# Sliding-window attention into a squared-ReLU MLP on one core: group 3 by seven products, one exponential a score bank, wider masks and sums, and a new order list

## The chip, the core and the metric

The kernel runs on one core of one Trainium2 chip. The metric is device time in microseconds (us): the median of several executions, and for one profiled execution also its span, from the first to the last instruction that the profile shows. The engines are named as in the profile: PE (TensorE, matmul), PEld (its weight loads), DVE (VectorE), ACT (ScalarE), POOL (GpSimd, here the issuer of the loads that cast) and SP (SyncE, here the issuer of the DMA transposes and of the stores).

## What is computed

The attention has 8 batches, 8 heads, 576 positions and head size 64, with a linear distance bias per head and a window of 128 positions. Its output, 4608 tokens of width 512, goes through an MLP of width 2048 with a squared ReLU. Inputs and output are float32.

```python
scores = scale * np.matmul(q, k.transpose(0, 1, 3, 2))
rel = pos[:, None] - pos[None, :]
bias = slopes[:, None, None] * (-np.abs(rel).astype(np.float32))[None, :, :]
mask = (rel >= 0) & (rel < window)
scores = np.where(mask, scores + bias[None], -1000000000.0)
...
attn = np.exp(scores)
attn = attn / (np.sum(attn, axis=-1, keepdims=True) + 1e-09)
return np.matmul(attn, v).astype(np.float32)
...
h = x @ w_in
r = np.maximum(h, 0.0)
g = r * r
return (g @ w_out).astype(np.float32)
```

## The kernel before, in words

**Blocks and groups.** The tokens are cut into 36 blocks of 128 queries (0 to 35; blocks 14, 21, 28 and 35 hold the last 64 positions of two batches). Each block goes through attention and leaves 128 columns of `xT`, the transposed input of the MLP. Four blocks make a group of 512 tokens; there are nine groups (0 to 8), and group g needs blocks 4g to 4g + 3. The first eight blocks are the first 128 positions of the batches and see only themselves.

**One block.** POOL loads K and Q (task `lkq`, `load_block`, L540 to L548) and V (`lv`, L550) with a cast to bf16 into rings of 4 and 9 tiles. From block 8 on, SP transposes K and Q by DMA into a ring of 7 (`kqT`, L592); a tile of `kq` is free again when that transpose has landed. PE makes the scores (`s`, L676) into four PSUM banks. ACT takes the exponential (`e`, L711, and `ex`, L719), DVE multiplies by a mask that holds the bias and the window (`m`, L725 to L734). PE multiplies by V in two halves (`pv`, L835), DVE divides by the sums (`r`, `n`, L854 and L859), and from block 8 on SP transposes the result by DMA into `xT` (`x`, L866). In a full block the scores of one head have three strips of 64 columns in each half of the partitions. One `e` takes the two outer strips of two heads (256 columns), one `ex` the middle strip (128 columns), so a bank has two exponentials; the middle strip is copied to two places by the mask's multiplication, so four heads have two masks of 512 elements.

**The way up** (x times w_in, ReLU, square). Groups 0 to 2 go in pieces (`unit`, `u`, L982), group 3 in 16 steps of four matmuls with 512 columns (`fc_step`, `fc`, L1002). Groups 4 to 8 (`G_UP = 4`) take each of four units (256 of w_in's columns and their partners 1024 further on) by seven products in place of eight (`up_product`, `f`, L1087): each product is four matmuls with 256 columns, on sums and differences of w_in's parts (`us`) and of x's parts (`ut`). Two PSUM banks serve a unit: X takes products 1, 6, 7, 4 and Y takes 2, 5, 3. The bank of product 1 is copied to Y (`s1.g.u`, the seed), and product 2 adds onto it there. Copies of X and Y after products 6 and 5 are parked in SBUF (`s2`, `s5`), and DVE adds them later (`c22`, `c12`, L1112).

**The way down** (g times w_out) of group 0 is direct (`o`, L1172). Groups 1 to 8 have seven products of 2 x 8 matmuls with 256 columns (`product`, `p`, L1261) on sums of the squared tile (`S1` to `S4`, `prepare`, two halves of 1024 elements each, L1391). After product 1 its bank is copied to an SBUF tile (`s1`), and DVE adds product 2's bank to it (`c11`, L1319).

**Order.** Every instruction group is a named task. `ORDER` lists all tasks by hand; the program walks the list and emits them in that order, so each engine runs its tasks in the list's order and waits for what a task needs. A `+` behind a name takes the second engine that the task allows. `SLACK`, `FILL` and the prices of the tasks enter only how many filling matmuls stand in planned gaps of the first 30 us. PSUM's eight banks are four rings: `h` (2), `ox`, `oy` (1 each) and `a` (4).

Of the kernel before, what the change touches and what calls it, by code (L numbers as in the profile page):

```python
# [9 lines left out]
AF = mybir.ActivationFunctionType  # L10
# [10 lines left out]
N_PVH = 2  # L21
# [3 lines left out]
SLACK = {"kqT": 4500.0, "v": 2300.0, "x": 2700.0}  # L25
FILL = 0.7
# [4 lines left out]
TP, XP = "h", "h"  # L31
# [8 lines left out]
G_A = 8  # L40
XR = 12
OSB = 5
LAST = 128
G_UP = 4
# [6 lines left out]
UNSEEDED = ((7, 1), (7, 3))  # L51
SQ_G = 0
SIZE = {"kq": 4, "v": 9, "kqT": 7, "P": 3, "x": 6}
# [15 lines left out]
    o0.0.3 ev4.1.0 ws0.3 lv6 tp5.0 squ0.5.0 tp5.1 lkq8 ev5.0.0 o0.1.3 ev5.1.0+ mask1.1 mask1.3 mask0.1 mask0.5 tp6.0
    oe0.1.0+ s4 lv7 oe0.0.0+ o0.3.0 e4.0 ws1.0 lkq9 mask1.4 e4.3 tp6.1 o0.3.1 e4.1 ev6.1.0+ ev6.0.0 one0.7 o0.2.0  # L70
    m4.0 lv8 e4.2 m4.1 one1.8 m4.3 squ0.5.1+ pv4.0 tp7.0 m4.2 lkq10 tp7.1 r4.0 ev7.0.0 n4.0 pv4.1 kqT8 pv5.0 pv5.1
    ev7.1.0 o0.2.1 r5.0 r5.1 r4.1 n5.0 lkq11 n5.1 o0.3.2 st0.0.0 n4.1 s6 kqT9 xp5.0 lv9 e6.0 xp4.0 x5.0+ o0.2.2
    x4.0+ e6.3 lv10 one1.6 one1.0 m6.0 u1.0.0 e6.2 m6.3 e6.1 one0.6 u1.0.3 reluu1.0.0 m6.1 one1.3 m6.2 pv6.0 ws1.1
    u1.0.5 reluu1.0.3 lkq12 squ1.0.0 pv6.1 r6.0 u1.0.7 reluu1.0.5 n6.0 r6.1 us3.0 u1.0.6 n6.1 reluu1.0.7 squ1.0.5
    mask0.0 kqT11 pv7.0 squ1.0.7 pv7.1 reluu1.0.6 u1.0.2 us2.0 r7.1 squ1.0.3+ r7.0 n7.0 u1.0.1 squ1.0.6+ kqT10 n7.1
    reluu1.0.2 lkq13 o0.3.3 reluu1.0.1 squ1.0.2 mask0.6 xp6.0 mask0.2 s8 x6.0+ lv11 ws1.3 xp7.0 e8.0 u1.0.4 oe0.3.0+
    e8.3 lv12 ex8.1 x7.0 o0.2.3 one1.2 ex8.2 e8.2 reluu1.0.4 u1.1.1 st0.3.0 ws1.2 e8.1 st0.1.0 ex8.3 ws0.2 u1.1.4
    ex8.0 kqT12 reluu1.1.1 mask0.7 s9 squ1.1.1 reluu1.1.4 us3.1 u1.1.5 squ1.0.1 e9.0 m8.0 e9.2 oe0.2.0+ lkq14 ex9.3
    u1.1.0 ex9.0 reluu1.1.5 m8.1 ex9.1 squ1.1.4 p1.1.0 squ1.0.4+ m8.3 one1.4 m9.1 reluu1.1.0 u1.1.2 squ1.1.5 e9.1
    one1.1 m8.2 kqT13 squ1.1.0 pv8.0 reluu1.1.2 u1.1.3 r8.0 n8.0 ex9.2 e9.3 lkq15 u1.1.6 m9.2 reluu1.1.3 m9.0 S1.1.0  # L80
# [1378 lines left out]
```

## Time and profile before

| what | value |
|---|---|
| median of the runs | 291.29 us (290.59 to 291.85, 3 runs) |
| the profiled execution, its own time | 292.82 us |
| its span | 290.6 us |
| PE busy | 282.0 us, 97% |
| PEld, weight loads | 231.2 us, 80% |
| DVE busy | 233.6 us, 80% |
| ACT busy | 212.3 us, 73% |
| POOL busy | 103.9 us, 36% |
| moved by DMA | 39.67 MB, mean 137 GB/s |

The busy time of an engine leaves overlaps of its own instructions out; the mean time of one instruction in the lists by line does not, so many of them times their mean is more than their busy time. The chain that ended last is followed back from the last instruction, at each step to what released it. A wait is put down to the engine or DMA that came last.

### The profile page before, as it was taken

To read this page: it belongs to the slowest core of one execution; us is meant where nothing else is said; L and a number is where in the kernel's file an instruction comes from. 1 tells how busy PE (TensorE), PEld (TensorE's weight loads), DVE (VectorE), ACT (ScalarE), POOL (GpSimd) and SP (SyncE) were. 2 spreads that over 40 slices of the span, in tenths; PEclk is the share of its full clock that TensorE was granted. 3 is DMA by queue.
4 is the path that set the end of the run, shared out by engine and by line. 5 is a ranking of instruction groups with operands and counts; after the bars stand their busy time and mean duration, and the time that the engine had idled before them with its cause. 6 is when DMAs were issued, how large, how long until landed. Compare 5 with 4: busy or idle time off the path is not lost.

```text
span 290.6 us, 9452 instructions
## 1 busy us (share of the span) xinstructions
PE 282.0 (97%) x3785; PEld 231.2 (80%) x3785; DVE 233.6 (80%) x628; ACT 212.3 (73%) x521; POOL 103.9 (36%) x132
## 2 busy tenths in 40 slices
PE   8899999999999999999899999999999999999994
PEld 4678746888888987558788889898888988888884
DVE  4554187789958897878799999999999996989853
ACT  3766765887479873778579899899989867675820
POOL 8942497448470434624717097340000000000000
PEclk9999999999999999999999999999999999999999
DMA  8999999999999999999999999999830201300144
GB/s 147 161 198 205 203 168 156 181 179 155 151 170 142 132 153 145 158 144 171 157 182 151 187 165 126 165 167 244 131 71 25 76 18 38 126 2 0 56 117 138
DMA packets 159915, 39.67 MB, mean 137 GB/s; under 512 B 142336, under 2 KB 159360, under 8 KB 159872
## 3 DMA queue, kind: packets, MB, share of 16 engines
q0 software_dynamic: 104432, 18.10, 88.8%
q1 hardware_dynamic: 54640, 20.33, 44.0%
q10 hardware_dynamic: 800, 0.66, 0.8%
q8 instruction: 29, 0.48, 0.7%
q14 instruction: 14, 0.11, 0.1%
HBM read 36.70 MB, written 9.44 MB: 159 GB/s over the span
## 4 chain that ended last, share of the span: by engine, by line
PE 78%; DMA 15%; DVE 2%; ACT 1%; POOL 1%; issue 1%; POOLq 0%; DVEq 0%
PE o L1261 27%; PE h L1087 19%; PE h L982 12%; DMA vt<-in_v_dram 8%; DMA kqT<-kq 7%; PE o L1172 5%; PE pv L835 5%; PE s L676 4%; PE h L1002 1%; PE wm L575 1%; PE tp L608 1%; POOL kq L546 1%; ACT kqf L403 1%; PE o L1348 1%; PE s L781 1%
## 5 line engine op out<-in xcount | busy, mean ns | idle before, releaser
L938 ACT ACTIVATE rt<-h 128x512 bf16<-128x512 f32 (+1 forms) x103 | 60.6, 594 | 26.1 <-PE h L982 9.0
L1261 PEld LDWEIGHTS <-g 128*128 128x128 bf16 x624 | 59.6, 98 | 7.8
L1261 PE MATMUL o<-w_out_sb,g 128*128 128x256 bf16 x512 | 63.6, 273 | 0.0
L711 ACT ACTIVATE P<-s 128x256 bf16<-128x256 f32 (+1 forms) x120 | 46.6, 426 | 11.0 <-PE s L676 11.0
L546 POOL DMA_DIRECT2D kq<-in_k_dram x32 | 27.1, 850 | 67.8 <-DMA kqT<-kq 67.0
L982 PE MATMUL h<-xT,w_in_sb 128*128 128x256 bf16 (+1 forms) x432 | 46.6, 261 | 0.2 <-ACT rt L938 0.2
L953 DVE TENSOR_TENSOR g<-rt 128x512 bf16<-128x512 bf16 (+1 forms) x85 | 34.6, 416 | 11.6 <-ACT rt L938 11.5
L982 PEld LDWEIGHTS <-w_in_sb 128*128 128x128 bf16 x432 | 37.4, 98 | 5.5 <-issue 0.3
L951 ACT ACTIVATE g<-rt 128x512 bf16<-128x512 bf16 (+1 forms) x60 | 36.6, 624 | 3.6 <-DVE rt L1120 3.2
L1087 PE MATMUL h<-xT,w_in_sb 128*128 128x256 bf16 x240 | 34.4, 273 | 0.0
L1087 PEld LDWEIGHTS <-w_in_sb 128*128 128x128 bf16 x320 | 30.4, 98 | 4.1 <-issue 0.3
L1261 PE MATMUL o<-wsum,sums 128*128 128x256 bf16 x256 | 31.1, 273 | 0.0
L552 POOL DMA_DIRECT2D vt<-in_v_dram x32 | 27.2, 868 | 9.0 <-PE pv L835 7.5
L859 DVE TENSOR_TENSOR x<-pv,rec 128x256 bf16<-128x256 f32 x72 | 28.5, 416 | 0.9
L835 PEld LDWEIGHTS <-P 128*128 128x128 bf16 x544 | 23.4, 98 | 5.7 <-DMA vt<-in_v_dram 1.4
L546 POOL DMA_DIRECT2D kq<-in_q_dram x32 | 27.4, 863 | 0.0
L1261 PEld LDWEIGHTS <-sums 128*128 128x128 bf16 x256 | 24.7, 98 | 3.0
L403 ACT ACTIVATE osb<-o 128x512 f32<-128x512 f32 x29 | 17.3, 602 | 11.4 <-DMA out_dram<-osb 5.3
L719 ACT ACTIVATE P<-s 128x128 bf16<-128x128 f32 x96 | 24.1, 304 | 0.0
L1112 DVE TENSOR_TENSOR rt<-h,vf 128x512 bf16<-128x512 f32 x30 | 20.5, 688 | 4.2 <-PE h L1087 1.9
L1087 PE MATMUL h<-ut,kqf 128*128 128x256 bf16 x160 | 23.5, 273 | 0.0
L835 PE MATMUL pv<-vt,P 128*128 128x65 bf16 x416 | 21.2, 193 | 1.7 <-DMA vt<-in_v_dram 1.5
(97 smaller groups left out, 462.0 us busy)
## 6 DMA issues: line engine op xcount, KB each, us to landing
out_dram<-osb SPq DMA_DIRECT2D x53, 128.0 KB, 3.9
kq<-in_k_dram POOLq DMA_DIRECT2D x31, 128.0 KB, 7.1
kq<-in_q_dram POOLq DMA_DIRECT2D x31, 128.0 KB, 7.2
vt<-in_v_dram POOLq DMA_DIRECT2D x24, 128.0 KB, 7.5
w_out_sb<-in_moe_w_out_dram POOLq DMA_DIRECT2D x4, 512.0 KB, 14.8
w_in_sb<-in_moe_w_in_dram POOLq DMA_DIRECT2D x3, 512.0 KB, 12.1
vf<-in_v_dram POOLq DMA_DIRECT2D x8, 128.0 KB, 6.2
out_dram<-osb SPq DMA_DIRECT2D x4, 256.0 KB, 6.6
```

What stands on the lines that cost most here:

```text
L546: nc.gpsimd.dma_start(view(kq[s_kq[m].idx], i)[rows], from_)
L552: nc.gpsimd.dma_start(tile_of(s_v[m])[rows, :, 0:D], from_)
L711: nc.scalar.activation(o, s, AF.Exp, bias=0.0, scale=scale)
L719: nc.scalar.activation(Pt[sP.idx][:, w, 1, early], s, AF.Exp, bias=0.0, scale=scale)
L835: nc.tensor.matmul(sv.tile[:, hi * (D + 1):(hi + 1) * (D + 1)], prob, tile_of(s_v[mk])[:, h, 0:D + 1], start=mk == parts[0][2], stop=mk == m)
L859: nc.vector.tensor_tensor(o, heads(sv)[:, :, 0:D], sr.tile.unsqueeze(2).to_broadcast([n, 4, D]), op=ALU.mult)
L938: nc.scalar.activation(srt.tile[:, 0:n], slot.tile[:, 0:n], AF.Relu, bias=0.0, scale=1.0)
L951: nc.scalar.activation(o, i, AF.Square, bias=0.0, scale=1.0)
L953: nc.vector.tensor_tensor(o, i, i, op=ALU.mult)
L982: nc.tensor.matmul(slot.tile[:, f * w:(f + 1) * w], w_in_sb[:, cc, fc * 128:(fc + 1) * 128], xT[:, cc, lo % (XR * 128):lo % (XR * 128) + w ...
L1087: nc.tensor.matmul(slot.tile[:, j * 256:j * 256 + 256], a, b_, start=fresh and j == 0 and c == 0, stop=c == 1, skip_group_check=True)
L1261: nc.tensor.matmul(slot.tile[:, z * 256:z * 256 + 256], stationary(c), moving(c), start=fresh and z == 0 and c == 0, stop=c == F - 1, skip ...
```

## The change

- `G_UP` goes from 4 to 3: group 3 goes up by seven products too, six groups in all.
- A full block's scores go through one exponential of 384 columns a bank, all three strips at once, into a raw tile of the new ring `E` (2 tiles). One multiplication for four heads then reads the raw tile twice over (the view `strips`: columns 0 to 127 and 64 to 191 of each head), multiplies by both masks and writes 1024 elements to `P`. `P` has 2 tiles instead of 3, `osb` 4 instead of 5. `ex` is gone.
- The sums `S1` to `S4` of groups 1 to 7 are made whole (2048 elements) in place of two halves; group 8 keeps the halves.
- Way down: product 1's bank is copied to the second PSUM bank, and product 2 adds onto it; `c11` becomes a copy out of that bank. All units of the way up are seeded (`UNSEEDED` is gone).
- The four PSUM rings become eight single banks. A task that takes a bank of kind `any` has its number behind a colon in the list; score blocks with four banks take banks 4 to 7.
- The list is new throughout (1676 tasks in place of 1814), with it the order of POOL's loads and SP's transposes and stores.

The core of the diff, and of the list the places that the text below speaks of:

```diff
-SLACK = {"kqT": 4500.0, "v": 2300.0, "x": 2700.0}
-FILL = 0.7
+SLACK = {"kqT": 3000.0, "v": 2300.0, "x": 1500.0}
+FILL = 0.85
...
-OSB = 5
+OSB = 4
...
-G_UP = 4
+G_UP = 3
...
-SIZE = {"kq": 4, "v": 9, "kqT": 7, "P": 3, "x": 6}
+SIZE = {"kq": 4, "v": 9, "kqT": 7, "P": 2, "E": 2, "x": 6}
...
-    n3.0 w_out2 e3.1 u0.0.1 x2.0+ pv3.1 u0.3.0 reluu0.0.1 r3.1 squ0.0.0+ n3.1 squ0.0.1 xp3.0 squ0.1.0 reluu0.3.0
...
-    r15.1 u2.1.5 n15.1 x14 squ2.1.0+ S1.2.1 s16 reluu2.1.1 S3.2.1 x15 p2.2.0 reluu2.1.5 S2.2.1 e16.0 p2.1.1 squ2.1.5
...
-    m18.2 fc3.0 r16.1 r16.0 n16.0 lkq26 pv17.0 m18.3 relufc3.0 fc3.7 r17.0 n17.0 n16.1 pv17.1 relufc3.7 fc3.5 r17.1
...
+    us0.2 S1.2.0 s15 s1_2:2 pv14.0:1 e15.0 pv14.1:0 S2.2.0 e15.2 p2.2.0 e15.1 e15.3 p2.2.1 r14.0 S3.2.0 s16 n14.0
+    p2.6.0 m15.1 r14.1 m15.0 e16.0 e16.1 e16.2 n14.1 p2.5.0:1 e16.3 pv15.0:5 pv15.1:6 us2.2 p2.6.1 m16.0 x14 r15.0
+    p2.5.1 lv21 n15.0 r15.1 n15.1 m16.1 x15 s17 s2_2 p2.7.0 p2.7.1 e17.0 S4.2.0 e17.2 c11_2 e17.1 lkq20 s5_2+ p2.3.0
+    c22_2 kqT19 kqT21 e17.3 pv16.0:0 r16.0 m17.1 s18 n16.0 p2.3.1 m17.0 e18.0 e18.2 c12_2 e18.3 p2.4.0 kqT23
+    pv16.1:4 m18.1 e18.1 r16.1 m18.0 pv17.0:5 pv17.1:0 n16.1 st2.2.0 st2.3.0 p2.4.1 s3_2 pv18.0:6 f3.0.1:7 f3.1.1:4
...
-    psum_bufs = {"h": 2, "ox": 1, "oy": 1, "a": 4}
+    psum_bufs = {f"b{i}": 1 for i in range(8)}
...
+    def strips(s):
+
+        e = Et[s.idx][:, :, 0:128].rearrange("p h (t q) -> p h t q", t=2)
+        return bass.AP(tensor=e.tensor, offset=e.offset, ap=[*e.ap[:-1], [1, 128]])
...
-        sS = [Slot("a") for _ in range(4)]
+        sS = [Slot(f"b{4 + i}") for i in range(4)]
...
+        sE = Slot("E" if full else "P")
+        sP, sR = Slot("P") if full else sE, Slot("E")
...
-            cols = 256 if (i % 2 and not diag) or kind == "full" else 512
+            cols = 384 if full else 256 if i % 2 and not diag else 512
...
+                s = sS[i].tile[:, 0:cols]
+                if full:
+                    o = Et[sE.idx][:, 2 * i:2 * i + 2].rearrange("p j q -> p (j q)")
...
-            if kind == "full":
-                def expo_x(i=i, w=w):
-                    s = sS[i].tile[:, 0:384].rearrange("p (c s q) -> p c s q", c=2, s=3)[:, :, 1]
-                    nc.scalar.activation(Pt[sP.idx][:, w, 1, early], s, AF.Exp, bias=0.0, scale=scale)
...
-                if i % 2:
-                    nc.vector.tensor_tensor(p[:, :, 1:3], p[:, :, 2:3].to_broadcast([128, 4, 2, 64]), mk[:, :, 1:3], op=ALU.mult)
-                else:
-                    nc.vector.tensor_tensor(p[:, :, 0:4:3], p[:, :, 0:4:3], mk[:, :, 0:4:3], op=ALU.mult)
+                nc.vector.tensor_tensor(Pt[sP.idx][:, g], strips(sE)[:, g], masks[:, g], op=ALU.mult)
...
-        fresh = p in (1, 2, 5)
+        fresh = p in (1, 5)
...
-        after = {6: "s1", 7: "s2", 3: "s5", 4: "c22"}.get(p)
+        after = {2: "s1", 6: "s1", 7: "s2", 3: "s5", 4: "c22"}.get(p)
...
         if p == 1:
-            snap("s1", [])
+            Y = st["slot"]["Y2"]
+
+            def seed():
+                bank(Y, "o")
+                copy(st["s1"], Y.tile, slot.tile)
+            st["s1"] = plan.add({"ACT": act(512), "DVE": dve_p(512)}, key, seed, both, [Y], [], name=f"s1_{g}")
         elif p == 2:
-            combine("s1", lambda o: nc.vector.tensor_tensor(o, slot.tile, o, op=ALU.add), both + [st["s1"]], [slot],
-                    0, 0, "c11")
+            snap("c11", [slot])
+            store("c11", st["c11"], 0, 0)
...
+        nq = 1 if g == NG - 1 else 2
+        for q in range(2 // nq):
+            qs = range(q * nq, q * nq + nq)
+            c, d = slice(4 * q, 4 * q + 4 * nq), slice(8 + 4 * q, 8 + 4 * q + 4 * nq)
```

The order of POOL's loads from block 16 on is, before: lkq16 lkq17 lkq18 lv15 lv18 lkq19 lkq23 lv16 lkq20 lv17 lkq21 lv19 lkq22 lv22 lkq26 lv20 lkq25 lkq24 lv21; after: lkq16 lv13 lv14 lkq17 lkq18 lv16 lv15 lv17 lv18 lkq19 lkq21 lv19 lkq23 lv21 lkq20 lkq22 lv22 lv20 lkq25 lkq26 lkq24.

More of the change, by code (lines that the diff above doesn't have):

```diff
@@ L262, in order @@
                     slots_at = max(slots_at, u[-n].freed)
-                    s.prev = u[-n]
+                if s.seed and not (u and u[-1].full):
+                    raise RuntimeError(f"{name}: its bank was not written as a whole before")
                 u.append(s)
@@ L1033 @@
     up_st = {}
-    t_parked, seeds = {}, []
+    t_parked = {}
     def prepare_up(g, key):
@@ L1422 @@
     kernel.plan = done
-    for X, Y in seeds:
-        if not (Y.prev and Y.prev.full):
-            raise RuntimeError("a bank is seeded that was not written as a whole before")
     with tc.manual_schedule():
```

355 lines of the change are left out of this document (170 added, 185 removed).

## The prediction

> **What bounds the kernel now.** I read the page first, to see which engine is never idle.
>
> ```profile
> span 290.6 us, 9452 instructions
> ...
> PE 282.0 (97%) x3785; PEld 231.2 (80%) x3785; DVE 233.6 (80%) x628; ACT 212.3 (73%) x521; POOL 103.9 (36%) x132
> ...
> DMA  8999999999999999999999999999830201300144
> ...
> PE 78%; DMA 15%; DVE 2%; ACT 1%; POOL 1%; issue 1%; POOLq 0%; DVEq 0%
> ```
>
> TensorE (PE) is busy for 282.0 of 290.6 us, but DMA is near full for the first 28 of 40 slices and holds 15% of the chain. So I ask, with busy time by stretch, where PE's missing 8.6 us lie.
>
> ```profile
> 0.00:20.00 20.00, 17.36 (x226) 12.06 (x227) 10.65 (x41) 11.80 (x28) 16.04 (x26) 1.00 1.30 165
> 80.00:100.00 20.00, 19.74 (x356) 17.04 (x355) 14.64 (x46) 17.00 (x47) 7.90 (x9) 1.00 1.75 157
> 100.00:120.00 20.00, 19.54 (x292) 14.65 (x288) 17.21 (x44) 12.66 (x40) 8.89 (x11) 1.00 2.21 136
> 140.00:160.00 20.00, 18.70 (x291) 16.10 (x290) 17.64 (x52) 14.96 (x41) 11.49 (x14) 1.00 1.96 163
> 160.00:180.00 20.00, 19.71 (x295) 16.93 (x294) 19.71 (x53) 18.84 (x52) 12.33 (x16) 1.00 1.73 162
> 240.00:260.00 20.00, 20.00 (x185) 17.93 (x184) 16.93 (x36) 15.04 (x29) 0.00 (x0) 1.00 0.20 61
> 280.00:290.60 10.60, 6.95 (x72) 6.16 (x69) 2.80 (x6) 2.25 (x4) 0.00 (x0) 1.00 0.43 128
> ```
>
> The columns are length, then PE, weight loads, VectorE (DVE), ScalarE (ACT), GpSimd (POOL), clock, DMA. PE lacks 2.64 us in the start, 3.65 in the end, and 0.26 + 0.46 + 1.30 + 0.29 = 2.3 between. The clock is 1.00 throughout. Does a busy PE mean a full PE? The chain of waits gives runs of matmuls without a gap:
>
> ```profile
> 71.20 0.47 PE s L676 x32
> ...
> 76.73 0.48 PE pv L835 x16
> 77.21 0.88 PE o L1261 x8
> ...
> 115.67 0.86 PE h L1002 x4
> ...
> 116.78 1.73 PE h L1002 x8
> ...
> 147.61 0.87 PE h L1087 x8
> ```
>
> Eight matmuls with 256 columns take 0.87 us (0.109 each), four with 512 take 0.86 (0.216 each): the array is streaming. The kernel is bound by the number of columns that PE streams, plus about 2.6 us of start and 2.3 us of waits.
>
> ```profile
> L1087 PEld LDWEIGHTS <-w_in_sb 128*128 128x128 bf16 x320 | 30.4, 98 | 4.1 <-issue 0.3
> ```
>
> A weight load takes 98 ns and fits under either pitch; in 240 to 260 us the loads are busy 17.93 of 20, 98 of each 109 ns.
>
> The Trainium skill, "Perfetto Trace Analysis", section "Identifying the Most-Contended Engine", says to judge PE's headroom by the busy share of weight loads and not of matmuls. By that rule 80% would leave a fifth; the pitches above leave almost nothing, since a 512-column matmul covers its load twice over.
>
> **The change, part by part.**
>
> *Group 3 by seven products.* Sixteen steps of four 512-column matmuls become four units of seven products with four 256-column matmuls: 64 x 0.216 = 13.8 us against 112 x 0.109 = 12.2. **-1.6 us** of PE, on the path.
>
> The Trainium skill, "TensorE: Matmul & The Clock Gate", section "Back-to-back issue gap", speaks against this: in a stream of load-matmul pairs it gives about 81 ns for 128 columns and 131 for 512. On a straight line that is an estimate of 98 ns for 256, and group 3 would go from 8.4 to 11.0 us, 2.6 us dearer. The rows above (0.216 and 0.109) disagree, so I keep -1.6.
>
> *Exponentials, masks, sums, copies.*
>
> ```profile
> L711 ACT ACTIVATE P<-s 128x256 bf16<-128x256 f32 x104 | 38.1, 399 | 8.8 <-PE s L676 8.8
> L719 ACT ACTIVATE P<-s 128x128 bf16<-128x128 f32 x96 | 24.1, 304 | 0.0
> L711 ACT ACTIVATE P<-s 128x512 bf16<-128x512 f32 x16 | 9.0, 600 | 2.1 <-PE s L676 2.1
> L732 DVE TENSOR_TENSOR P<-P,masks 128x512 bf16<-128x512 bf16 x48 | 19.6, 418 | 2.9 <-ACT P L719 2.8
> L734 DVE TENSOR_TENSOR P<-P,masks 128x512 bf16<-128x512 bf16 x48 | 19.6, 416 | 3.6 <-ACT P L711 3.6
> L1391 DVE TENSOR_TENSOR sums<-g 128x1024 bf16<-128x1024 bf16 x16 | 11.0, 685 | 0.5 <-ACT g L951 0.2
> L1319 DVE TENSOR_TENSOR osb<-o,osb 128x512 f32<-128x512 f32 x8 | 5.4, 678 | 0.1
> L403 ACT ACTIVATE h<-h 128x512 f32<-128x512 f32 x16 | 9.4, 588 | 5.9 <-PE h L1087 5.3 <-DVE rt L1120 0.4 <-DVE rt L1112 0.2
> L1112 DVE TENSOR_TENSOR rt<-h,vf 128x512 bf16<-128x512 f32 x30 | 20.5, 688 | 4.2 <-PE h L1087 1.9 <-ACT g L951 0.8 <-ACT vf L403 0.6
> L1120 DVE TENSOR_SCALAR rt<-rt 128x512 bf16<-128x512 bf16 x27 | 7.9, 298 | 0.2
> ```
>
> ACT: 96 pairs of 399 + 304 ns become 96 instructions with 384 columns. None is in the trace; it lies between the 256 and the 512 form (399 and 600), and I take the middle, 500. That is 67.5 - 48 = 19.5 us less by durations; by busy totals, which leave overlaps out (38.1 x 96/104 + 24.1 = 59.3 against 96 x about 0.465 = 44.6), 14.7. Added: the eight c11 copies that move to ACT, and one more 512-wide instruction in group 3 (8 relus and 9 copies for 16 relus), 9 x 0.6 = 5.4. ACT net about -9 us.
>
> DVE: 96 masks of 0.417 become 48 of 1024 elements; their nearest row is the 1024-wide sum, 0.685: 39.2 - 32.9 = -6.3. The new operand reads overlapping strips; at half the speed (417 grows by 269 ns per 512 more, so about 1.2 us) they would cost 48 x 0.54 = +26 instead. I take 0.685, since the old masks already read 64-wide strips, one of them repeated, at 417, the same as whole tiles. Sums of groups 1 to 7: 28 pairs of 0.685 become 28 of about 1.22, -4.1. The eight c11 additions leave, -5.4. Group 3 adds eight additions at 0.688, eight relus at 0.298, four differences at about 0.42 and three copies that the list gives DVE, about 2.1: +11.7. DVE net about -4.
>
> What are these worth? **0**: neither engine sets the end, and PE hides them while there is other PE work in line. A gain is bounded by PE's waits on them (below). A loss: a 2048-wide sum is ready 0.54 us later, and product 5 waits for it; products 1 and 2 (4 x 0.87 = 3.5 us) stand ahead and cover the two sums (2.4). Without that cover it is about 1 us in each of seven groups.
>
> *Product 2 of the way down is seeded.* It now waits for a copy of 0.59 us after product 1; in the queue behind it stands all later PE work. The new list puts other work between: least in group 2, where s15, pv14.0 and pv14.1 (0.47 + 2 x 0.36) cover it; at the end p7.4 (1.74) does. I take **+0.2**, bounds 0 and 7 x 0.6.
>
> *The list and named banks.* Here PE's waits go or come.
>
> ```profile
> PE pv L835 <- DMA vt<-in_v_dram: 1.5, 2, 1.3
> ...
> PE xp L879 <- ACT kqf L403: 0.5, 1, 0.5
> ...
> PE pv L835 <- DVE P L734: 0.3, 1, 0.3
> ```
>
> ```profile
> 133.06 11.27 DMA vt<-in_v_dram
> ```
>
> ```profile
> 144.37 0.48 PE L835 MATMUL pv<-vt,P 128*128 128x65 bf16 x10 [1.30 <-DMA vt<-in_v_dram]
> ```
>
> The load of block 21's values was issued at 133.06, behind K and Q of blocks 26, 25 and 24 on POOL's queue, and PE stood still 1.30 us for it until 144.37. In the new list lv21 stands before lkq20, lkq22, lkq25, lkq26 and lkq24, and lv16, lv17 also move up. **-1.5**; bounds 0 and -1.8 with the mask's wait.
>
> At the start, xp1 waited 0.5 us for ACT to empty the transposes of block 3; now tp3 and its copies come after the first unit. **-0.5**, bounds 0 and -1.4 (2.64 less the 1.23 before the first matmul).
>
> Against that stand the transposes of x. Group 3 needs block 15. In the old list 11 products, two score blocks and two pv halves (11.0 us) stand between x15 and fc3.0; in the new one six products, two score blocks and five pv halves: 6 x 0.87 + 2 x 0.47 + 5 x 0.24 = 7.4 us.
>
> ```profile
> 100.03 4.74 SPq L866 DMA_TRANSPOSE xT<-x  x2
> ```
>
> ```profile
> 114.09 1.02 PE L1002 MATMUL h<-xT,w_in_sb 128*128 128x512 bf16 x4
> ```
>
> ```profile
> DMA to landing us min/median/max: 8.7/10.1/10.7
> ```
>
> ```profile
> DMA to landing us min/median/max: 4.8/7.1/8.7
> ```
>
> x14 and x15 took SP's queue 4.74 us together from 100.03, 2.4 each, and the group began at 114.09, late enough for any landing. In the new list x14 stands just ahead of x15, whose turn I put 0.3 us later for it: 7.1 us are left. The two lower rows are the landings of x in 90 to 125 and in 125 to 160 us. With 8.7 PE waits 1.6 us at the head of group 3, with 10.7 it is 3.6, with 7.1 none. I take **+1.6**: fewer K and Q loads are pending there. Groups 4 and 5 have 8.3 and 8.6 us (seven and eight products, two score blocks, the pv halves at 0.24 or 0.36) against 7.1, at most 8.7: **+0.2**. That work can be earlier at other places of the list I can't price: 0.
>
> **Sum**: -1.6 + 0.2 - 1.5 - 0.5 + 1.6 + 0.2 = -1.6. Of the small PE stalls under 0.5 us inside score blocks and pv (0.26 + 0.46 + 0.29 = 1.0 in the stretches above) I count half as gone with the shorter exponential chain: -0.5. In all **-2.1 us**: the span goes from 290.6 to 288.5. The profiled execution took 292.82 us, 2.2 around its span; the median of the runs is 291.29, so I set the change against that: **289.2 us**.
>
> **The rivals.**
>
> *The waits come back (no change).* DMA is full in 28 of 40 slices, to 203 us, so PE may lose the same time to it wherever the list puts its work: the 1.5 returns at another block and x15 costs 3.6. -2.1 + 1.5 + 2.0 = +1.4 at the most, -0.35 at half: 290.9 to 292.7. For it: landings of 10 us. Against: PE lost only 1.5 us to data.
>
> *Transposes of x too late (slower).* One mechanism, at the heads of groups 3, 4 and 5: landings stay at 10.7 us. PE waits 3.6 + 2.4 + 2.1 = 8.1 where I counted 1.8: +4.2, **295.5 us**. With landing L the waits are 3L - 24; the change gains nothing at L = 9.3 and is slower by 0.5% at 9.8. For it: 8.7 to 10.7 before 125 us. Against: at most 8.7 behind it, and a wait at one head gives the next more time.
>
> *Half-speed masks.* 26 us more on a DVE that is busy 19.71 of 20 in 160 to 180 us: over 300 us.
>
> *Weight loads set the pitch.* If group 3's matmuls went at the pace of their loads, 64 x 98 ns = 6.3 us would become 112 x 98 = 11.0, +4.7 instead of -1.6: 291.29 - 2.1 + 1.6 + 4.7 = 295.5. The 0.216 us of the wide form, over twice its load, speaks against it. The page of the Trainium skill named above has a rule of this kind; by its figures the time would be 293.4, an estimate.
>
> **How the numbers follow.** A measurement of this kernel can tell about 0.5%, 1.5 us: faster is under 289.8, slower over 292.7. The forecast (287 to 289.8) gets 0.48, waits that return 0.22, late transposes 0.25, half-speed masks 0.03, loads that set the pitch 0.02. So faster 0.48, same 0.22, slower 0.30. Likeliest case alone: 286.8 to 289.8. Its low end is all gains at their bounds without x's wait: -1.6 - 1.8 - 1.4 = -4.8, 286.5. The range needs part of the late case: to 294.5.
>
> **What would show it.** Right: 112 matmuls at 256 columns in group 3 in place of 64 at 512, PE's busy time near 280; exponentials of 384 columns near 500 ns, masks near 685; no wait of pv for vt at 143; a wait of 1 to 3 us for xT at the first product of group 3. Wrong: masks near 1.2 us, waits of PE for xT at several heads, waits of product 2 for its copy, or PE idle between 20 and 280 us of over 4 us.

## The result, and the profile after

| kernel | median, runs | ratio to before, 95% interval |
|---|---|---|
| before, on the same chip | 291.32 us (290.59 to 291.85, 4) | 1 |
| changed | 294.83 us (294.23 to 295.25, 4) | 1.0121 (1.0091 to 1.0150) |

The change makes the kernel 3.5 us slower, where 2.1 us faster was forecast; the time lies 0.3 us over the range. The page of the changed kernel, as that of before was shown: span, busy times, the clock and DMA rows in 40 slices, and the chain's shares.

```profile
span 292.4 us, 9410 instructions
...
PE 281.1 (96%) x3832; PEld 235.8 (81%) x3837; DVE 234.3 (80%) x570; ACT 207.3 (71%) x429; POOL 104.1 (36%) x132
...
PEclk9799999999999999999999999999999999999999
DMA  8999999999999999999999999999944112210123
...
PE 86%; DVE 9%; ACT 2%; issue 1%; POOL 1%; DVEq 0%; POOLq 0%; ACTq 0%
```

PE is busy 0.9 us less than before and the span is 1.8 us longer. (Two further profiles of the kernel before, below, have PE busy for 281.0 and 281.1 us, so these 0.9 us are no saving that can be told.) DMA has left the chain (15% before, under 1% now); DVE has come in with 9%. The second slice of the clock shows a 7. Busy time by stretch, same columns as before (length, PE, weight loads, DVE, ACT, POOL, clock, DMA):

```profile
0.00:20.00 20.00, 15.54 (x192) 10.44 (x195) 9.38 (x40) 11.52 (x30) 15.41 (x25) 0.91 1.32 164
80.00:100.00 20.00, 20.00 (x301) 17.91 (x299) 14.95 (x44) 13.80 (x29) 8.59 (x11) 1.00 1.70 166
100.00:120.00 20.00, 19.83 (x352) 17.15 (x351) 17.43 (x39) 11.78 (x27) 6.94 (x9) 1.00 2.00 137
120.00:140.00 20.00, 19.53 (x246) 16.47 (x247) 19.50 (x43) 16.38 (x33) 8.80 (x10) 1.00 1.80 164
140.00:160.00 20.00, 19.02 (x305) 16.07 (x305) 17.66 (x48) 13.90 (x29) 11.22 (x14) 1.00 2.08 166
160.00:180.00 20.00, 18.77 (x317) 15.87 (x316) 18.39 (x40) 13.53 (x30) 8.22 (x12) 1.00 1.49 161
280.00:292.40 12.40, 8.58 (x86) 7.54 (x84) 3.52 (x7) 2.18 (x4) 0.00 (x0) 0.96 0.33 96
```

Two places lost time: the start (15.54 of 20 us, 17.36 before) and 100 to 180 us (2.85 us not busy). The waits of PE name the releasers; the columns are total, times, longest.

```profile
PE s L774 <- ACT sums L456: 1.6, 1, 1.6
...
PE tp L376 <- DVE kqf L400: 0.9, 1, 0.9
PE o L1249 <- DVE g L1384: 0.9, 1, 0.9
PE pv L830 <- DVE P L728: 0.5, 2, 0.4
PE o L1249 <- ACT osb L402: 0.5, 1, 0.5
```

No wait of PE for a DMA is in this list, and none for `xT`. Behind the last row stands one all the same. Product 7 of group 3 waited there for a parked copy (`s2_3`), and ACT, before it made that copy, waited 2.25 us for a store that still held an `osb` tile, of which there are now four and not five:

```profile
141.92 0.60 ACT L402 ACTIVATE osb<-o 128x512 f32<-128x512 f32 x1 [2.25 <-DMA out_dram<-osb]
```

A second profile of the changed kernel (`after_again`, below) does not have this wait; five tiles were not tried in the new list.

The first two rows are the start. There the new list differs from the old in a way that the prediction passed over: `b0`, the matmuls that write block 0's biases into PSUM (L774), needs all eight `slope` tiles (L454 on DVE, L456 on ACT). The list now has it ahead of `tp0.0`, the first transposes of K and Q (L610), and deals five slopes to ACT, four before. The timeline of the changed kernel (start, length, in brackets the idle time before and its releaser):

```profile
4.06 1.28 ACT L456 ACT_TABLE_LOAD   x1 [4.06 <-DVE sums L430]
5.35 1.11 ACT L456 ACTIVATE sums<-sums 128x128 bf16<-128x128 f32 x5
6.51 0.59 PE L774 MATMUL s<-sums,ident 128*128 128x512 bf16 x2 [1.55 <-ACT sums L456]
6.94 0.39 PE L610 MATMUL tp<-ident,kq 128*128 128x128 bf16 x4
7.36 0.38 ACT L402 ACTIVATE kqf<-tp 128x256 bf16<-128x256 bf16 x1 [0.90 <-PE tp L610]
7.78 0.42 DVE L400 COPY kqf<-tp 128x256 bf16<-128x256 bf16 x1 [2.87 <-ACT kqf L402]
...
10.30 0.61 PE L784 MATMUL s<-kqf 64*128 64x128 bf16 x8
```

The same steps in the kernel before:

```profile
4.93 0.63 PE L611 MATMUL tp<-ident,kq 128*128 128x128 bf16 x4
5.35 0.91 ACT L457 ACTIVATE sums<-sums 128x128 bf16<-128x128 f32 x4
6.53 0.96 PE L781 MATMUL s<-sums,ident 128*128 128x512 bf16 x2
8.39 0.40 PE L791 MATMUL s<-kqf 64*128 64x128 bf16 x8
```

ACT makes no slope before its table load ends at 5.34, PE stands for the fifth until 6.51, and the transposes, which need none, come behind it at 6.94 (4.93 before). `b0` itself runs at the same time in both kernels (6.51 and 6.53). The first scores come at 10.30, 8.39 before.

### The profile page after: what moved, and what is told of

Its sections match the earlier page's. It is cut to its first block, busy times and chain, and to the rows that moved or that the text cites. A ratio compares the mean times of both kernels' runs of the same rounds, so it can differ in the third digit from the quotient of the medians.

```text
span 292.4 us, 9410 instructions
## 1 busy us (share of the span) xinstructions
PE 281.1 (96%) x3832; PEld 235.8 (81%) x3837; DVE 234.3 (80%) x570; ACT 207.3 (71%) x429; POOL 104.1 (36%) x132
## 4 chain that ended last, share of the span: by engine, by line
PE 86%; DVE 9%; ACT 2%; issue 1%; POOL 1%; DVEq 0%; POOLq 0%; ACTq 0%
PE o L1249 28%; PE h L1079 23%; PE h L977 15%; PE pv L830 6%; PE o L1160 5%; PE s L680 4%; DVE P L728 2%; PE tp L607 2%; DVE g L1384 1%; DVE rt L1104 1%; DVE sums L1384 1%; PE xp L874 1%; DVE g L948 1%; PE s L774 1%; PE o L1341 1%
## 5 line engine op out<-in xcount | busy, mean ns | idle before, releaser
L933 ACT ACTIVATE rt<-h 128x512 bf16<-128x512 f32 (+1 forms) x97 | 55.9, 596 | 11.3 <-PE h L1079 5.6
L715 ACT ACTIVATE E<-s 128x384 bf16<-128x384 f32 x96 | 41.3, 498 | 10.7 <-PE s L680 10.5
L977 PE MATMUL h<-xT,w_in_sb 128*128 128x256 bf16 (+1 forms) x432 | 44.8, 261 | 0.0
L977 PEld LDWEIGHTS <-w_in_sb 128*128 128x128 bf16 x432 | 37.7, 98 | 4.2
L1079 PE MATMUL h<-xT,w_in_sb 128*128 128x256 bf16 x288 | 40.2, 273 | 0.2 <-DVE vf L400 0.2
L1079 PEld LDWEIGHTS <-w_in_sb 128*128 128x128 bf16 x384 | 36.4, 98 | 4.9 <-issue 0.4
L946 ACT ACTIVATE g<-rt 128x512 bf16<-128x512 bf16 (+1 forms) x55 | 34.2, 631 | 1.3 <-DVE rt L1112 0.7
L728 DVE TENSOR_TENSOR P<-E,masks 128x1024 bf16<-128x1024 bf16 x48 | 32.1, 679 | 3.3 <-ACT E L715 2.9
L1079 PE MATMUL h<-ut,kqf 128*128 128x256 bf16 x192 | 27.5, 273 | 0.0
L830 PEld LDWEIGHTS <-P 128*128 128x128 bf16 x512 | 21.9, 98 | 3.3 <-DVE P L728 1.1
L1104 DVE TENSOR_TENSOR rt<-h,vf 128x512 bf16<-128x512 f32 x32 | 21.7, 682 | 2.1 <-ACT vf L402 0.9
## 6 DMA issues: line engine op xcount, KB each, us to landing
w_out_sb<-in_moe_w_out_dram POOLq DMA_DIRECT2D x4, 512.0 KB, 12.7
```

The source lines that it names most:

```text
L715: nc.scalar.activation(o, s, AF.Exp, bias=0.0, scale=scale)
L728: nc.vector.tensor_tensor(Pt[sP.idx][:, g], strips(sE)[:, g], masks[:, g], op=ALU.mult)
L830: nc.tensor.matmul(sv.tile[:, hi * (D + 1):(hi + 1) * (D + 1)], prob, tile_of(s_v[mk])[:, h, 0:D + 1], start=mk == parts[0][2], stop=mk == m)
L933: nc.scalar.activation(srt.tile[:, 0:n], slot.tile[:, 0:n], AF.Relu, bias=0.0, scale=1.0)
L946: nc.scalar.activation(o, i, AF.Square, bias=0.0, scale=1.0)
L977: nc.tensor.matmul(slot.tile[:, f * w:(f + 1) * w], w_in_sb[:, cc, fc * 128:(fc + 1) * 128], xT[:, cc, lo % (XR * 128):lo % (XR * 128) + w ...
```

## The experiments

Ratios are to the kernel before on the same chip in the same hour; 0.001 is 0.29 us. Line numbers of runs whose list was edited can be 2 lower than those of the changed kernel.

### The prices the prediction took from one execution: the kernel before again

`b_again` and, later, `b_again2` are the kernel before, unchanged, for two more profiles.

> The kernel before, unchanged, for a second trace. Its profiled execution on record took 292.82 us where its runs have a median of 291.3. If the 1.5 us between them is the wait for block 21's values at 143 us, this trace shows a span near 289.5 and no wait of pv for vt over 0.5 us. If that wait is in every execution, it shows 1.3 us again at the same place.

> The kernel before once more, for a third profile. If the wait of block 21's values for their V (1.3 us), which the prediction counted as gone, is that one execution's, it isn't here: no wait of a probability product for the V tile over 0.3 us, span 288 to 289.5. If it is the kernel's, it is here again in at least this one of two further profiles.

They took 290.35 us (span 288.1) and 290.69 us (span 288.5). The wait of a probability product for V and the busy time over 100 to 200 us, of `b_again`:

```profile
PE pv L835 <- DMA vf<-in_v_dram: 0.3, 1, 0.3
```

```profile
100.00:200.00 100.00, 99.70 (x1481) 80.50 (x1480) 92.99 (x248) 81.75 (x218) 45.75 (x57) 1.00 1.78 164
```

and of `b_again2`:

```profile
PE pv L835 <- DMA vt<-in_v_dram: 0.4, 1, 0.4
```

```profile
100.00:200.00 100.00, 99.34 (x1476) 79.94 (x1475) 92.51 (x248) 81.17 (x216) 45.98 (x57) 1.00 1.88 164
```

The 1.30 us wait of block 21, worth -1.5 in the sum, is in neither. In these two the kernel before loses 0.3 to 0.7 us in this stretch, not 2.1. Both executions were faster than the median, so the wait is not one that every execution has; how often it comes is not shown. The execution that the prediction read was also 0.5 us late at the start: its first scores come at 8.39 us, at 7.86 and 7.85 in these two.

### The head of the list

`a_start` moves one task of the changed kernel:

```diff
-slope0.0 b0:36 tp0.0:2 ev0.0.2 lv1 ev0.0.0+ cq0
+slope0.0 tp0.0:2 ev0.0.2 lv1 ev0.0.0+ b0:36 cq0
```

> The changed kernel with one move at the start: b0 (the bias matmuls, which wait for all eight slopes) behind the first half of block 0's transposes instead of ahead of it. Theory: PE lost 1.8 us more than before in the first 20 us because the transposes stood behind b0; the move gives most of it back: 1.5 to 2.0 us less, 293.0. Rival: the start is held by loads and ACT anyway, and the first unit starts at 16.0 us as it does now: 294.8, within 0.4.

Measured: 292.61 us, 1.0027 (0.9995 to 1.0059): 2.2 us back. `a_start2` takes the old head whole, slopes four and four:

```diff
-slope0.3+ slope0.1+ slope1.0 slope1.2 slope1.1 slope1.3+ slope0.2 ck0 lv0 slope0.0 b0:36 tp0.0:2 ev0.0.2 lv1 ev0.0.0+ cq0 w_in0
+slope1.2+ slope0.1 slope0.0+ slope1.1 slope1.0 ck0 slope0.2 lv0 slope1.3+ tp0.0:2 ev0.0.2+ w_in0 slope0.3+ b0:36 cq0 lv1 ev0.0.0+
```

> The changed kernel with the head of the list as it stands in the kernel before: eight slopes dealt four to VectorE and four to ScalarE, the first transposes and their copy ahead of the bias matmuls. The theory that the start took about 2 us holds only if this comes at least as early as the run with the bias matmuls moved alone (292.6): in that run TensorE still waited 1.1 us for ScalarE's last slope. Theory 'the rest of the start is that wait': 291.6 to 292.3, TensorE busy in the first 20 us 17.0 to 17.4 (16.6 there), no wait of the bias matmuls for ScalarE over 0.5 us. Rival 'that wait is covered by the next one, the copy of the transposes': 292.4 to 293.0, busy 16.5 to 16.7.

> The changed kernel with the head of before once more (291.9), for a trace at full clock beside the run with the two moves alone: 291.4 to 292.4, the product's wait for its sum 0.7 to 1.0 us in the trace, TensorE busy in the first 20 us 17.3 to 17.6.

Measured: 291.87 us, 1.0014 (0.9987 to 1.0041), and 292.27 us, 1.0040 (1.0008 to 1.0073). The second's start, and the wait that matters below:

```profile
0.00:20.00 20.00, 17.53 (x232) 12.06 (x235) 10.22 (x42) 12.96 (x32) 15.98 (x26) 1.00 1.31 164
```

```profile
PE o L1247 <- DVE g L1382: 0.9, 1, 0.9
```

The wait for ACT's slopes is gone, and PE is busy 17.53 of 20 us, where before has 17.1 to 17.4, though part of this is filling (below). By ratio the old head whole (mean 1.0027) gives no more than `b0` moved alone (1.0027), where PE still waited 1.1 us for ACT's last slope. That the dealing of the slopes costs time is therefore not shown. `after_again`, the changed kernel once more, stands beside them:

> The changed kernel once more beside the others of this call, so that what mending the head and the order gave back stands on one chip: 294.2 to 295.2, TensorE busy in the first 20 us 15.3 to 15.7, the wait of the bias matmuls for ScalarE's slopes 1.5 to 1.7 us, the product's wait for its sum 0.8 to 1.0.

It gave 294.27 us, 1.0107 (1.0072 to 1.0141), with the two start waits at 1.8 and 0.9. From the means of the two ratios each, 1.0114 and 1.0027, the head costs 2.5 us in the new list, by the intervals with about 1 us either way. Does it cost that by itself? `b_head` puts it into the kernel before:

```diff
-slope1.2+ slope0.1 slope0.0+ slope1.1 slope1.0 ck0 slope0.2 lv0 slope1.3+ tp0.0 one0.1 ev0.0.2+ w_in0 slope0.3+ b0 cq0 lv1 ev0.0.0+
+slope0.3+ slope0.1+ slope1.0 slope1.2 slope1.1 slope1.3+ slope0.2 ck0 lv0 slope0.0 b0 tp0.0 one0.1 ev0.0.2 lv1 ev0.0.0+ cq0 w_in0
```

> The kernel before with nothing of the change but the head of the new list: the bias matmuls of block 0 ahead of its first transposes, five of the eight slopes on ScalarE. Theory 'the head alone costs what mending it gave back' (2.2 us for the place of the bias matmuls, 3.0 with the dealing of the slopes): 293.3 to 294.5, TensorE busy in the first 20 us 14.5 to 15.6 (17.1 to 17.4 before). Rival 'the head costs that only beside the rest of the new start, which moves more work ahead of the first scores': 291.0 to 292.0.

> The kernel before with the head of the new list once more, since its first ratio (1.0019, 0.9984 to 1.0054) leaves open whether the head costs 0 or 1.5 us there. Theory 'the head costs in before what its trace shows, 1.5 us': 292.3 to 293.0. Rival 'it is covered in before': 291.0 to 291.6.

Measured: 291.87 us, 1.0019 (0.9984 to 1.0054), and 292.29 us, 1.0050 (1.0028 to 1.0071). My theory missed the first: the head costs 0.6 to 1.5 us there, not 2.2 or more. The first scores are late there too. Those of `b_head`:

```profile
10.32 0.54 PE L789 MATMUL s<-kqf 64*128 64x128 bf16 x8
```

They come at 9.70 us in `b_head_again`, at 7.85 to 8.39 in the three profiles of before. Is the new start packed more tightly, so that less of a delay can vanish in its waits? PE from 10 to 20 us in `b_again` and in `a_best_again` (below, new list with the old head):

```profile
10.00:20.00 10.00, 8.67 (x146) 6.80 (x146) 6.58 (x25) 7.42 (x17) 7.69 (x11) 1.00 1.57 188
```

```profile
10.00:20.00 10.00, 9.54 (x166) 7.65 (x166) 5.36 (x19) 9.26 (x24) 7.31 (x11) 1.00 1.59 184
```

It looks so, with 9.54 us busy against 8.67. But the matmuls that fill planned gaps count as busy. Here they are alone (length, PE, weight loads), in the same order:

```profile
10.00:20.00 10.00, 0.56 (x4) 0.24 (x4) 1.00 1.57 188
```

```profile
10.00:20.00 10.00, 1.74 (x19) 1.12 (x19) 1.00 1.59 184
```

Without them PE is busy for 8.1 us in the old start and 7.8 in the new one, so the new start is not fuller with work. What does differ on record is how long PE ran at half clock: with the new head to 11.3 us or later in the new list, to 9.7 and 5.5 us in the two runs of `b_head` (last section). That fits a larger price in the new list; no run isolates it.

### The order on VectorE between 100 and 180 us

The product's wait of 0.9 us for its sum has a cause in the queue. DVE and PE in `a_start2_again`:

```profile
171.33 0.69 DVE L726 TENSOR_TENSOR P<-E,masks 128x1024 bf16<-128x1024 bf16 x1 [1.26 <-ACT E L713]
...
171.94 1.22 DVE L1382 TENSOR_TENSOR g<-g 128x2048 bf16<-128x2048 bf16 x1
...
173.21 1.92 PE L1247 MATMUL o<-w_out_sb,g 128*128 128x256 bf16 x16 [0.87 <-DVE g L1382]
```

DVE stands 1.26 us for ACT ahead of a mask (`m26.1`), and the sum that PE needs (`S3.4.0`, 1.22 us, inputs long there) is queued behind it. `a_best` has the old head and moves two DVE steps:

```diff
-m25.1 p4.6.0 p4.6.1 s27 lkq32 e27.0 c11_4 p4.3.0 pv24.1:4 m26.1 S3.4.0 p4.3.1
+m25.1 S3.4.0 p4.6.0 p4.6.1 s27 lkq32 e27.0 c11_4 p4.3.0 pv24.1:4 m26.1 p4.3.1
...
-c12_4 ut5.0 n24.1 lv27 m27.1 f5.0.1:7
+c12_4 m27.1 ut5.0 n24.1 lv27 f5.0.1:7
```

> The head of the list as before, and two moves on VectorE: the third sum of group 4 ahead of a mask of block 26 that stands idle for ScalarE there (1.26 us), and the last mask of block 27 ahead of two steps that are due later. Theory 'small waits in the middle come from the order on VectorE': the product's 0.9 us wait for the sum and the 0.36 us wait for the mask go, 290.4 to 291.2. Rival 'they come from VectorE's whole load in that stage': the waits move to the next users and the time stays within 0.4 us of the run with the head alone.

> The run with the mended head and the two VectorE moves once more (290.9, ratio 0.9989, 0.9964 to 1.0014), to narrow whether it beats the kernel before. Theory of the prediction with its start and its order mended (1.6 us of TensorE work less in group 3): 289.6 to 290.4, ratio 0.995 to 0.998. Rival 'the group's saving is taken back by the small waits between 100 and 200 us': 290.7 to 291.3, ratio 0.999 to 1.001.

Measured: 290.91 us, 0.9989 (0.9964 to 1.0014), and 291.20 us, 0.9997 (0.9963 to 1.0030). 160 to 180 us in `a_best`:

```profile
160.00:180.00 20.00, 19.72 (x307) 17.04 (x305) 19.53 (x42) 13.73 (x30) 10.23 (x13) 1.00 1.72 169
```

PE is busy for 19.72 of 20 us, 18.77 in the changed kernel. The product's wait for its sum and the 0.36 us wait for the mask are gone; a new one of 0.3 us, for a normalisation on DVE, has come. By ratios the two moves are worth 1.0 us with the old head. Of what `a_best_again` was to decide, the rival came true: 0.9997 and 291.20 us lie in its ranges, so the saving of group 3 does not show in the time. `a_moves` keeps the new head and makes only the two moves:

> The changed kernel with its own head and only the two VectorE moves. Theory 'the head costs about 3 us in the new list, and the two moves about 1, and the two add up': 293.3 to 294.1, TensorE busy in the first 20 us 15.3 to 15.7, no wait of a product for its sum over 0.3 us. Rival 'the head's delay is made up further on once the order on VectorE is mended': 291.0 to 292.4.

Measured: 293.28 us, 1.0093 (1.0057 to 1.0129). Against `a_best` and `a_best_again` (mean 0.9993) the head is 2.9 us, and against the changed kernel (1.0114) the moves are 0.6 us, so head and order about add up. Two further moves, in `a_best2` (the last normalisation of block 24 ahead of `ut5.0`, and a parked copy of group 3 from DVE to ACT: `s2.3.2+` becomes `s2.3.2`) and in `a_best3` (the first of them alone):

> The run with the head and two VectorE moves (290.9), with two moves more: a parked copy of group 3 from VectorE to ScalarE, ahead of which TensorE stood 0.4 us, and the last normalisation of block 24 ahead of an addition of group 5, for which a probability product stood 0.3 us. Theory 'each of the small waits left is one step's place': 290.2 to 290.7, both waits gone. Rival 'group 3 by seven products holds VectorE and ScalarE full from 118 to 134 us, so a wait that goes there comes back at the next user': 290.7 to 291.2, TensorE busy 120 to 140 still 19.5 or less.

> The same, with the last normalisation of block 24 ahead of an addition of group 5, and the parked copy left on VectorE. The run with both moves gave 291.3 and a new wait of 0.6 us for the copy on ScalarE. Theory 'that copy made it worse, the normalisation is a gain': 0.2 to 0.4 us below the run beside it, the probability product's 0.3 us wait gone. Rival 'no gain, the next user waits': within 0.2 us of it.

Measured: 291.29 us, 0.9996 (0.9964 to 1.0027), and 290.95 us, 1.0004 (0.9979 to 1.0030), 0.25 us below `a_best_again` beside it, which its ratio does not bear out. The copy on ACT made a wait of its own (of `a_best2`):

```profile
PE h L1077 <- ACT vf L400: 0.6, 1, 0.6
```

The small waits are at the grain where one goes and another comes.

### Each part of the change alone

`a_fc3` sends group 3 up by 16 steps of 512 columns again (`G_UP = 4`), in the places of its products:

```diff
-G_UP = 3
+G_UP = 4
```

> The changed kernel with group 3 up in 16 steps of 512 columns again, put at the places of its seven products in the list. Theory: PE streams 1.6 us more, and that is the result: +1.2 to +2.0, 296.4. Rival: group 3's extra additions and copies on a DVE that is busy 19.5 of 20 in 120 to 140 us cost more than PE saves; without them the time falls, to 294 or less.

Measured: 296.17 us, 1.0155 (1.0108 to 1.0203), 1.2 to 1.3 us over the changed kernel. The intervals of the two overlap, and PE is idle for 3.45 us between 100 and 200 us in this run, for 2.3 to 2.9 in the changed kernel; its way up also begins later, at 17.00 us against 16.03 and 16.75. So the time alone does not show the group's saving. PE's own time does. Counted from the start of one matmul to the start of the next, with idle time left out, the way up of groups 3 to 8 takes 76.7 us in `a_fc3` and in the kernel before, and 74.9 to 75.4 in the changed kernel and the runs with its list: 1.3 to 1.8 us less, about as forecast.

`a_half` makes the sums of groups 1 to 7 in halves again (`nq = 1`, each `S` of the list twice):

> The changed kernel with the sums S1 to S4 of groups 1 to 7 in two halves again, each half right behind the other in the list. Theory: whole sums come late for the products (PE waited 0.9 us for one at 176 us); the first halves let the products begin 0.6 us earlier: 0.5 to 1.5 us less, 294.0. Rival: DVE has no room, and 28 more instructions cost it 28 x 0.07 = 2 us in stretches where it is full: no gain or up to 1 us slower.

Measured: 294.17 us, 1.0090 (1.0054 to 1.0127): within 0.7 us of the changed kernel by medians, 0.7 by mean ratios. The intervals overlap, and neither expectation is decided. `a_undo` is `a_start` with the old number of exponentials and masks:

```diff
+                if full:
+                    o, s = (y.rearrange("p (c s q) -> p c s q", c=2, s=3) for y in (o, s))
+                    nc.scalar.activation(o[:, :, 0:3:2], s[:, :, 0:3:2], AF.Exp, bias=0.0, scale=scale)
+                    nc.scalar.activation(o[:, :, 1], s[:, :, 1], AF.Exp, bias=0.0, scale=scale)
+                    return
...
-                nc.vector.tensor_tensor(Pt[sP.idx][:, g], strips(sE)[:, g], masks[:, g], op=ALU.mult)
+                for y in (slice(g.start, g.start + 2), slice(g.start + 2, g.stop)):
+                    nc.vector.tensor_tensor(Pt[sP.idx][:, y], strips(sE)[:, y], masks[:, y], op=ALU.mult)
```

> The run with the bias matmuls moved alone (292.6), with the exponential of a bank as two instructions (256 and 128 columns) and the mask of four heads as two of 512 columns, as in the kernel before; nothing else. VectorE gains 48 instructions of about 0.16 us each and ScalarE 96 of about 0.25. Theory 'the single exponential and the wide masks are worth what they take off VectorE and ScalarE in the stages where these bind': 293.2 to 294.5. Rival of the prediction, that they are worth nothing on the path: 292.3 to 292.9.

Measured: 293.27 us, 1.0065 (1.0039 to 1.0092), 0.7 us over `a_start` by medians, 1.1 by ratios. The two intervals overlap, but the time lies in the range of the theory and outside the rival's. The single exponential and the wide masks look like a gain of about that size in this list, not 0.

`a_thin` and `a_best_thin` leave the squares of groups 3 and 4 (3, 4 and 5) out of `a_start` and `a_best`; the ReLU of these groups writes straight to the squared tile. The first of three places in `a_thin`:

```diff
+            if g in (3, 4):
+                nc.scalar.activation(in_g(g, out_of), slot.tile[:, 0:n].rearrange("p (f t) -> p f t", f=2), AF.Relu, bias=0.0, scale=1.0)
+                return
```

> The run with the bias matmuls moved alone (292.6), without the squares of groups 3 and 4: their relu writes straight to g, which takes 32 instructions off VectorE and ScalarE (0.42 and 0.63 us each) in the two stretches where TensorE is not full (120 to 140, 160 to 180 us); the values of these groups differ. Theory 'VectorE and ScalarE bound the up stage by seven products, and its backlog delays the sums behind': TensorE busy in both stretches at 19.7 or more (18.9 and 18.8 there), time 290.0 to 291.0. Rival 'the order of the list or the banks makes the waits': both stretches within 0.3 us of before, time 292.2 to 293.0.

> The run with the head and the two moves (290.9), without the squares of groups 3, 4 and 5 (their relu writes straight to g; the values of these groups differ). Theory 'what is left between 100 and 200 us, 1.3 us of TensorE not busy, comes from VectorE and ScalarE being full in the up stages by seven products, group 3's among them': 289.3 to 290.2, TensorE busy 99.5 or more of the 100 us. Rival 'the banks and the list's order make it': 290.6 to 291.2, TensorE busy 98.5 to 99.0.

`a_thin`: 291.79 us, 1.0017 (0.9994 to 1.0041), under `a_start` by 0.8 us by medians and 0.3 by ratios. Of the two stretches that were to tell load from order, 120 to 140 us fills up, from 18.87 us of PE in `a_start`, and 160 to 180 us stays as it was (18.76):

```profile
120.00:140.00 20.00, 19.87 (x293) 17.14 (x292) 17.37 (x31) 12.91 (x26) 9.99 (x12) 1.00 1.74 166
160.00:180.00 20.00, 18.77 (x297) 16.19 (x296) 17.78 (x39) 12.19 (x27) 10.23 (x13) 1.00 1.79 178
```

So the later stretch was order, which `a_best` then mended, and not load. The earlier one speaks for load, by one profile each; the changed kernel itself has 19.53 there and `a_best` 19.51. `a_best_thin`: 289.97 us, 0.9972 (0.9946 to 0.9998). Its 100 to 200 us, and those of `a_best`:

```profile
100.00:200.00 100.00, 98.77 (x1543) 85.19 (x1541) 88.75 (x196) 66.09 (x138) 45.43 (x55) 1.00 1.80 163
```

```profile
100.00:200.00 100.00, 98.71 (x1537) 84.27 (x1536) 96.09 (x223) 75.24 (x156) 44.40 (x54) 1.00 1.86 157
```

7.3 us less of DVE work and 9.2 of ACT work leave PE's 1.2 to 1.3 us of idle time where they were. The time came 0.9 us lower by medians (0.5 to 0.7 by ratios). That lies in the range of the theory (289.3 to 290.2), while PE's 98.77 us lie in the rival's, and the trace does not show where the time went. That the rest of the waits is load is not borne out.

Not tried alone were the named banks, the smaller rings (`P`, `osb`), the seed of product 2, and `SLACK` and `FILL`.

## Why the prediction was wrong, point by point

- **The start, -0.5: wrong in sign.** The step looked at one wait of the old start (`xp1`, 0.5 us) and asked whether the new list drops it. It does, but others come. The step did not follow the new list from its first task, where `b0` now stands ahead of `tp0.0`. With its own head the new list is 2.5 to 2.9 us slower than with the old one; this is the largest part of the error. Even with the old head the forecast gain does not show: of the first 20 us PE is then busy for 13.8 to 14.2 without the filling matmuls, and for 14.1 to 14.4 in the three profiles of before. Nor was the clock 1.00 throughout, as the prediction read it (last section).
- **The wait of block 21, -1.5: not a wait of every execution.** It is in one profile of before, whose own time (292.82) stood 1.5 us over the median; that was the sign. Two further profiles have 0.3 and 0.4. Setting a wait of one execution against the median of the runs was the mistake.
- **Half of the small stalls, -0.5: wrong in sign.** PE's loss between 100 and 200 us is 0.3 to 0.7 us in the two further profiles of before and, in the changed kernel, 2.85 (2.27 in `after_again`, 97.73 of 100 busy). Of this, 0.6 to 1.0 us is the order of DVE's steps, shown by two moves, and 0.52 in the one profile is the wait behind the `osb` tile. With both moves 1.2 to 1.8 us stay in every variant, and their cause is open. The prediction had a wait of that kind, a whole sum 0.54 us later, and priced it 0 since products 1 and 2 cover it. They do cover it; what waited was product 7, for `S3`, queued behind a mask.
- **`x15` late, +1.6: did not come.** The turns of x14 and x15, a product of group 3 later, in the changed kernel:

```profile
L861 SPq DMA_TRANSPOSE xT<-x x2: 1190/1354/1519, 107.5 to 109.6; - x2
...
DMA to landing us min/median/max: 7.7/8.2/8.7
```

```profile
117.69 1.47 PE L1079 MATMUL h<-xT,w_in_sb 128*128 128x256 bf16 x12
```

  x15 went out at 109.56 us, 8.1 ahead of its first use and not 7.1, and landed 7.7 later, at 117.29; x14 took 8.7 and landed before it. PE shows no wait, by a margin of 0.4 us. Lead and landing were within 1 us of the numbers used, but the term took the longer landing and the shorter lead. The rival built on it (295.5) came near the time by another way, which is luck.
- **Group 3, -1.6: right** in PE's time on the way up (1.3 to 1.8 us less), and the pitch with it; weight loads did not set it. It did not reach the end: PE's busy time as a whole did not fall (below).
- **The prices of instructions: right.** By line and form, in the changed kernel:

```profile
L715 ACT ACTIVATE E<-s 128x384 bf16<-128x384 f32 x96 | 41.3, 498 | 10.7 <-PE s L680 10.5 <-DVE P L728 0.2
L728 DVE TENSOR_TENSOR P<-E,masks 128x1024 bf16<-128x1024 bf16 x48 | 32.1, 679 | 3.3 <-ACT E L715 2.9 <-PE pv L830 0.3
L1384 DVE TENSOR_TENSOR sums<-g 128x2048 bf16<-128x2048 bf16 x7 | 8.5, 1214 | 0.1
```

  498, 679 and 1214 ns for 500, 685 and 1220. The totals came out otherwise: DVE's busy time went from 233.6 to 234.3 us where -4 was forecast, ACT's from 212.3 to 207.3 where -9 was. The sums set durations of single instructions against busy time, which leaves overlaps out. The worth of 0 on the path looks too low: by `a_undo` it is 0.7 to 1.1 us.
- **The seed of product 2, +0.2**: no wait for its copy of 0.2 us or more is in the list.

The sum, as the runs have it: head +2.5 to 2.9, order on DVE +0.6 to 1.0, the rest -0.1 (mean ratio of the four mended runs, `a_best` to `a_best3`, 0.9997). That rest should hold group 3's saving, and PE's busy time shows what became of it: 281.0 and 281.1 us in the two further profiles of before, 281.1, 281.1, 282.1 and 282.0 in the four mended runs. Counted from start to start, the way up is 1.3 to 1.5 us shorter there, but the filling matmuls, 38 where 25 were, take 0.6 to 1.1 us more, and the products on the way down of groups 1 to 8 take 0.9 to 1.2 us more, for a cause that stays open. Idle time between 100 and 200 us adds 0.6 to 1.5. Against that, the time outside the span is 1.8 us with the changed kernel's code and 2.2 before, and this too is unexplained. No variant that does all the work is measurably faster than the kernel before.

## What to carry to other kernels

Walk a new order list from its first task, engine by engine, with the times at which each engine can begin: here one task that waits 1.6 us stood ahead of one that need not wait, and the list with that head lost 2.5 to 2.9 us, more than the whole gain that was forecast. A wait seen in one profile should not be priced in full until a second shows it, above all when that execution stands over the median. Take filling matmuls out of PE's busy time before two starts are compared. On an engine as full as DVE here (18.4 of 20 us), a step that waits for another engine sets back every finished-input step behind it, so put what PE needs next ahead of it.

## What was not expected of the hardware

Every profile here begins at half clock, though the clock column says 1.00 there, since its records begin later. The pitch of the matmuls shows it. `b0`'s two matmuls with 512 columns take 0.96 us in the kernel before and 0.59 in the changed one (rows above), and in `a_half` the first and the third pair of this kind take:

```profile
6.51 1.01 PE L774 MATMUL s<-sums,ident 128*128 128x512 bf16 x2 [1.40 <-ACT sums L456]
...
14.42 0.59 PE L774 MATMUL s<-sums,ident 128*128 128x512 bf16 x2
```

By the pitch and the trace's clock records, the full clock comes at 5.7 to 7.3 us in the three profiles of before, at 3.9 to 7.2 in the new list with `b0` behind the transposes, and at 9.7 and 5.5 in `b_head` and `b_head_again`. With the new head in the new list (five profiles) it stays only from 11.3 to 14.4 us on. In `a_half` and `a_fc3` it first comes at 13.9 and 13.1. In the changed kernel, twice, and in `a_moves` it comes at 4.2 to 4.7 us, falls back to half after 3.4 us and returns 3.4 to 6.8 us later. In the first:

```profile
4.66:8.08 3.42, 1.11 (x10) 0.63 (x9) 0.55 (x2) 2.17 (x7) 3.42 (x5) 1.00 1.53 180
8.08:11.49 3.41, 2.90 (x34) 2.15 (x34) 1.79 (x11) 1.04 (x4) 3.41 (x5) 0.50 1.68 147
```

In the 3.4 us before the three falls PE was busy for 1.11, 1.36 and 1.20 us; in the profiles that kept the full clock, the first 3.4 us of it were busy for 1.61 us (`b_head_again`) or more. No single idle stretch was over 1.8 us. The Trainium skill, "TensorE: Matmul & The Clock Gate", section "What's actually happening", puts the drop behind an idle window of about 3.4 us; here a window that was a third busy was enough.

The half clock costs time at the start. In the five profiles of the new list with the new head PE ran at half clock for 6.7, 6.9, 9.8, 11.9 and 12.7 us in all (`a_moves`, changed, `after_again`, `a_fc3`, `a_half`), and the first matmul of the way up came at 15.93, 16.03, 16.75, 17.00 and 17.09 us. So part of the head's price may be the clock and not the wait itself; how much, no run isolates.
